# A table load placed ahead of a transfer on ScalarE, and a 1.5 KB transfer moved back in the load queue

## The chip, the core and the metric

One core of a Trainium2 chip runs the kernel, in one launch. The core has five instruction streams that matter here: PE (matrix products and transposes), ACT (ScalarE), DVE (VectorE), POOL (GpSimd) and SP, which only issues transfers. ACT and POOL issue transfers too, from the same stream that gives them their arithmetic. All transfers are carried out by the same 16 DMA engines.

The metric is the device time of one execution in microseconds (us). Three executions of the kernel before took 119.38, 119.49 and 120.67 us, a median of 119.49.

## What is computed

Two stages in one kernel. The first is a linear attention with a decaying state, for 4 batches, 8 heads, 768 steps and a head size of 48. The second takes its output as 3072 rows of 384 and runs a soft mixture of experts (8 experts of 4 slots, hidden size 1024).

```python
# attention: r, k, v are (4, 8, 768, 48); w, u are (8, 48)
for t in range(S):
    cur = einsum('bhd,bhe->bhde', u[None] * k[:, :, t], v[:, :, t])
    y[:, :, t] = einsum('bhd,bhde->bhe', r[:, :, t], state + cur)
    state = w[None, :, :, None] * state + einsum('bhd,bhe->bhde', k[:, :, t], v[:, :, t])
x = y.transpose(0, 2, 1, 3).reshape(3072, 384)
# soft mixture of experts
logits = x @ phi                                   # (3072, 32)
d = softmax(logits, axis=0); c = softmax(logits, axis=1)
slot_in = (d.T @ x).reshape(8, 4, 384)
slot_out[e] = relu(slot_in[e] @ w1[e]) @ w2[e]     # 8 experts
out = c @ slot_out.reshape(32, 384)
```

`w` and `u` are 1.5 KB each. `w` enters everything: its logarithm, times a position, is exponentiated into tables by which every k and r is scaled. `u` enters only the term of a step with itself.

## The kernel before, in words

**Tiling.** The 768 steps are cut into chunks of 128, and a batch is loaded in two parts: a small one (m even, 384 KB for each of k, r and v) and a large one (m odd, 768 KB each). So there are 24 loads, named `Lk0 Lr0 Lv0` to `Lk7 Lr7 Lv7`. Each goes into one of 14 buffers `raw`, all through one function, `load_f` (line 195), issued by SP. The expert weights, 16 matrices of 1.57 MB in float32, are later loaded into the same buffers by POOL (lines 783 and 785), which turns them into bfloat16 on the way, 768 KB each in SBUF. The first of these waits for a small copy (`gate`, line 781) that needs the load `Lk6`.

**The order of the work.** Nothing is scheduled at run time. The string `ORDER` (lines 9 to 31) names some 500 tasks, and `L.run(ORDER)` emits them in that order; each task puts its instructions at the end of its engine's stream, and each engine works its stream off in order. A name with `:ACT` or `:DVE` picks the engine. The first line of the string sets the start:

```python
CB0 Lk0 Sk0 Lr0 Tk0 Sr0 LU Lv0 Ek0:ACT VC0:ACT Lk1 AHa AHb F0_2 Tr0 Lr1 PR0 TB0b F1_3 N0 TB0a F2_2 Tv0 Ev0 Lv1 CC Lk2
```

The tasks that matter here are:

- `LU` (line 381): SP issues the load of `u` into `u_f`, 4 rows of 384 bytes. It stands behind `Lr0`.
- `Sk…`, `Sr…` (line 427): k or r times a table; the first two on DVE, most others on POOL.
- `T…` (line 436): PE turns a scaled tile; `E…` (lines 357 and 359): DVE or ACT copies it out of PSUM; `PR` (452): DVE multiplies; `N`, `V` (481, 491): PE turns tiles again.
- `AHa AHb` (line 281, DVE) and `TB…` (line 397, ACT): arguments and exponentials of the large tables. `Sk1b`, the first product on POOL, needs `TB0b`.
- `CC` (lines 291 to 293): DVE copies a small constant (`permT`), then `w_f`, then `u_f` into `wu`. `CT` (line 311): PE turns both, one transpose each. `CA` (314): DVE copies the result out. `CU` (317, 318; POOL) and `CW` (322, 324; ACT) make `ucol` and `wT` of it, which all later state updates use.
- `F…_n` (line 861): matrix products of n times 256 columns whose result nobody reads.
- The tail: `W15a`, `W15` (line 785) load the last weight matrix in two parts; `Q11`, `Q12`, `Q13` (line 921) are its products, behind which line 928 (ACT) and lines 949 to 955 make and store the output.

**Ahead of the tasks** stands a straight piece of code. ACT's stream begins with these two lines:

```python
O(act.dma_start(out=w_f, in_=w.rearrange("(o q e) d -> o q (e d)", o=1, e=2).to_broadcast([C // nQ, nQ, P2])))   # L211
O(act.preload_act_table_set("natural_log_exp_and_others"))                                                       # L212
```

The first issues the load of `w`, broadcast to 128 rows (48 KB). The second loads the function table that holds logarithm and exponential. Behind them ACT makes two permutation matrices of an identity that POOL writes (lines 255 and 260), then the logarithm of `w` (line 283), then DVE multiplies (281) and ACT exponentiates (287, 288). On PE, 2 and then 7 products on zeros (line 219) stand around two matrix products (266, 267) that need the permutation matrix of line 255.

**Waits of the load queue.** The transfers issued by SP and ACT share eight completion semaphores in turn. So each such transfer from the ninth on waits, ahead of its issue, for the landing of the one eight places before it. In the kernel before the first eight are w, k0, r0, u, v0, k1, r1, v1.

Of the kernel before, what the change touches and what calls it, by code (L numbers as in the profile page):

```python
# [6 lines left out]


ORDER = """
CB0 Lk0 Sk0 Lr0 Tk0 Sr0 LU Lv0 Ek0:ACT VC0:ACT Lk1 AHa AHb F0_2 Tr0 Lr1 PR0 TB0b F1_3 N0 TB0a F2_2 Tv0 Ev0 Lv1 CC Lk2  # L10
TB1b F3a_9 V0 CT Sk1b Sr1b Sk1a:DVE Lr2 Er0:ACT NE0:ACT CA F4a_11 Tk1b F5a_1 Tk1a VE0 A00 CB TB1a Ek1a VC1b VC1a:ACT
Lv2 CU K00 F6_4 Tr1b Tv1a Ek1b:ACT CW Ev1a Lk3 Sr1a F7y_1 U0 Er1b:ACT SM0 Sk2 N2 A01 K01 NE2:ACT Tv1b Sr2 Ev1b:ACT
Sk3a F8y_3 Tr1a SI0 Lr3 Lv3 N1 Sk3b Er1a:ACT Lk4 VC3b PR1b V1 A10 Sr3a DV0 VC2:ACT K10 Y0 NE1:ACT VE1:ACT Sr3b YE0 Tv2
# [68 lines left out]
def kernel(  # L82
# [31 lines left out]
    CC = NS // U3  # L114
# [11 lines left out]
    def O(ins):  # L126
        return tc.keep_in_program_order(ins)

    pe, dve, act, pool, sp = nc.tensor, nc.vector, nc.scalar, nc.gpsimd, nc.sync
# [78 lines left out]
    for t in wu_t:  # L208
        O(dve.memset(t[:], 1.0))

    O(act.dma_start(out=w_f, in_=w.rearrange("(o q e) d -> o q (e d)", o=1, e=2).to_broadcast([C // nQ, nQ, P2])))  # L211
    O(act.preload_act_table_set("natural_log_exp_and_others"))  # L212

    warm = LexpT[:, 0:512]
    O(dve.memset(warm, 0.0))
# [770 lines left out]
```

## Time and profile before

| what | value |
|---|---|
| median of three executions | 119.49 us |
| the profiled execution's own time | 120.24 us |
| its span, first to last instruction | 118.5 us |
| busy share of the span: PE, DVE, ACT, POOL | 83%, 80%, 73%, 52% |
| mean granted clock of PE | 0.962 |
| bytes read from and written to HBM | 39.42 MB, 4.72 MB |

The profile's rows give a start and a duration in us (ns where a row says mean ns), the engine, the line of the kernel, and what was written from what. An engine's name with a q behind it (SPq, ACTq) is its instruction stream, which issues transfers. "DMA share" is the mean busy share of the 16 DMA engines. Rates in GB/s count the bytes moved as written to SBUF; the weights are read as float32 and written as bfloat16, so half the rate stands for the same reading. Rows that end in a releaser in brackets tell how long the engine stood idle and what ended it.

### The profile page before, as it was taken

The page shows a single profiled execution, that of the slowest core. Times are in us where ns is not written, and L with a number is a line of the kernel's source. Part 1 is how long each engine was busy: PE and PEld are TensorE (multiplying, and loading weights), DVE is VectorE, ACT ScalarE, POOL GpSimd, SP SyncE. Part 2 cuts the span into 40 slices and gives each one's busy share as a digit, 9 for nine tenths or more (in the row PEclk, how much of TensorE's full clock was granted, in tenths as well). Part 3 has the DMA queues.
Part 4 walks back from the last instruction along what each step waited for, and adds up shares of the span by engine and source line. Part 5 has one row for each costly group of instructions (what it writes and reads, how often), then busy time and mean ns, then how long its engine had stood idle before and what let it go on. Part 6 is the DMA issues. An engine that isn't in the chain of part 4 may idle for free.

```text
span 118.5 us, 3926 instructions
## 1 busy us (share of the span) xinstructions
PE 98.0 (83%) x1660; PEld 71.1 (60%) x1660; DVE 94.8 (80%) x180; ACT 86.6 (73%) x140; POOL 61.0 (52%) x79
## 2 busy tenths in 40 slices
PE   3997895999999999989999989999899985498000
PEld 0364674787888787867788878686453542254000
DVE  6899987898999999999999989999786274099100
ACT  5769894999999999989899799979644151269000
POOL 7605899999999989999999010002303000000000
PEclk9999999999999999999999999999999999869955
DMA  2999999999999999999999999999999995059994
GB/s 31 333 387 374 364 408 397 383 390 401 384 384 391 297 229 223 219 215 214 217 212 221 210 223 207 223 207 219 212 212 218 216 207 104 12 199 407 419 402 166
DMA packets 10441, 31.81 MB, mean 268 GB/s; under 512 B 1080, under 2 KB 4408, under 8 KB 10424
## 3 DMA queue, kind: packets, MB, share of 16 engines
q0 software_dynamic: 2448, 12.58, 51.8%
q1 hardware_dynamic: 7832, 18.93, 42.3%
q8 instruction: 13, 0.21, 0.7%
q10 hardware_dynamic: 144, 0.05, 0.2%
q14 instruction: 4, 0.03, 0.1%
HBM read 39.42 MB, written 4.72 MB: 373 GB/s over the span
## 4 chain that ended last, share of the span: by engine, by line
PE 32%; DMA 23%; POOL 15%; DVE 9%; ACT 6%; issue 4%; SPq 3%; DVEq 0%; ACTq 0%; POOLq 0%
DMA raw<-in_moe_w_dram 16%; POOL mix L427 12%; PE T L436 7%; DMA raw<-in_r_dram 7%; PE Ab L506 3%; DVE mix L953 2%; PE Yb L572 2%; SPq L195 2%; PE T L491 2%; PE Yb L567 2%; DVE AT_all L511 2%; ACT xT_all L359 2%; PE Yb L578 2%; PE T L481 2%; PE T L595 2%
## 5 line engine op out<-in xcount | busy, mean ns | idle before, releaser
L427 POOL TENSOR_TENSOR mix<-raw,tabl 128x768 bf16<-128x768 f32 x15 | 27.7, 1858 | 5.8 <-ACT tabl L397 5.4
L511 DVE TENSOR_TENSOR AT_all<-Ab,mask 128x1024 bf16<-128x1024 f32 x24 | 29.3, 1219 | 1.1 <-PE Ab L506 0.5
L359 ACT COPY mix<-T 128x1024 bf16<-128x1024 bf16 x19 | 19.1, 1021 | 3.9 <-PE T L436 2.3
L436 PEld LDWEIGHTS <-mix 128*128 128x128 bf16 x192 | 11.8, 99 | 2.3 <-DVE mix L427 0.7
L555 DVE TENSOR_TENSOR dv<-vn,Mb 128x768 bf16<-128x768 bf16 x12 | 11.4, 946 | 1.4 <-PE Mb L545 1.1
L427 POOL TENSOR_TENSOR mix<-raw,tabs 128x768 bf16<-128x768 f32 x6 | 10.8, 1815 | 0.0
L359 ACT COPY vT_all<-T 96x1024 bf16<-96x1024 bf16 x10 | 10.2, 1021 | 0.5 <-PE T L436 0.4
L506 PE MATMUL Ab<-mix 64*128 64x128 bf16 x192 | 9.5, 218 | 1.2 <-ACT mix L359 1.0
L359 ACT COPY xT_all<-T 128x768 bf16<-128x768 bf16 (+1 forms) x12 | 9.3, 784 | 1.3 <-PE T L595 1.3
L359 ACT CAST x<-Yb 128x768 bf16<-128x768 f32 x12 | 9.7, 808 | 0.0
L436 PE MATMUL T<-turnl,mix 128*128 128x128 bf16 x128 | 9.6, 219 | 0.1
L359 ACT COPY vn<-T 128x768 bf16<-128x768 bf16 x11 | 8.8, 814 | 0.0
L452 DVE TENSOR_TENSOR pr<-T,mix 128x1024 bf16<-128x1024 bf16 x12 | 8.0, 681 | 0.0
L712 POOL TENSOR_TENSOR Lc<-Ls,sm 128x192 bf16<-128x192 f32 x2 | 1.0, 516 | 13.5 <-ACT E L690 13.5
L506 PEld LDWEIGHTS <-mix 64*128 64x128 bf16 x192 | 5.8, 94 | 3.5 <-issue 0.7
L572 PEld LDWEIGHTS <-AT_all 128*128 128x128 bf16 x192 | 6.6, 96 | 1.6
L359 ACT COPY kn<-T 128x768 bf16<-128x768 bf16 (+1 forms) x10 | 7.2, 722 | 0.1
L418 POOL CAST vj<-raw 128x768 bf16<-128x768 f32 x8 | 6.7, 832 | 0.6 <-POOL phi_s L336 0.6
L436 PEld LDWEIGHTS <-vj 128*96 128x96 bf16 x96 | 6.2, 123 | 1.2 <-issue 0.2
L572 PE MATMUL Yb<-vn,AT_all 128*128 128x48 bf16 x192 | 6.8, 183 | 0.0
L539 DVE TENSOR_TENSOR Z<-Mb,wT 128x384 bf16<-128x384 f32 x12 | 6.6, 553 | 0.1
L481 PE MATMUL T<-ident,mix 128*128 128x128 bf16 x80 | 6.1, 219 | 0.2
(187 smaller groups left out, 237.8 us busy)
## 6 DMA issues: line engine op xcount, KB each, us to landing
raw<-in_moe_w_dram POOLq DMA_DIRECT2D x13, 768.0 KB, 14.4
raw<-in_k_dram SPq DMA_DIRECT2D x4, 768.0 KB, 12.2
raw<-in_r_dram SPq DMA_DIRECT2D x4, 768.0 KB, 12.2
raw<-in_v_dram SPq DMA_DIRECT2D x4, 768.0 KB, 12.2
out_dram<-mix SPq DMA_DIRECT2D x3, 768.0 KB, 4.6
raw<-in_k_dram SPq DMA_DIRECT2D x4, 384.0 KB, 10.9
raw<-in_r_dram SPq DMA_DIRECT2D x4, 384.0 KB, 10.6
raw<-in_v_dram SPq DMA_DIRECT2D x4, 384.0 KB, 10.8
```

The lines of the kernel that those rows point to most:

```text
L195: O(sp.dma_start(out=dst[:, 0:2 * jn * D].rearrange("p (e x) -> p e x", e=2), in_=a[b].rearrange("h (y j) d -> y h (j d)", j=jn)[lg * CC * ...
L359: O(act.copy(dst, src))
L418: O(act.copy(o, i_) if t.eng == "ACT" else pool.tensor_copy(o, i_))
L427: O(eng.tensor_mul(src.inst.rearrange("p (j e s) -> p e j s", j=JH, e=2)[:, :, :, 0:D], rv(), tab))
L436: O(pe.transpose(Tb.inst[0:P, jj * 128:(jj + 1) * 128], sv[:, jj, :], (turn, turnl)[lg][:]))
L452: O(dve.tensor_mul(cv(pb), tv(), cv(kT)))
L481: O(pe.transpose(Tb.inst[:, x * 128:(x + 1) * 128], kT.inst[:, x, :], ident[:]))
L506: O(pe.matmul(Abf.inst[:, e, x * C:(x + 1) * C], kT.inst[s, g * nQ + x, :], rT.inst[s, g * nQ + x, :]))
L511: O(dve.tensor_mul(AT.inst[:], Abf.inst[:].rearrange("p e (g t) -> p e g t", g=nQ), mask[:, None, None, :].to_broadcast([128, 2, nQ, C])))
L539: O(dve.tensor_mul(Smid.inst[:], Mf.inst[:, 0:SW].rearrange("p (q d) -> p q d", q=nQ)[:, :, None, :].to_broadcast([128, nQ, 2, D]), wT[:, ...
L555: O(dve.tensor_mul(dvb.inst[:].rearrange("p g e d -> p (g e) d"), vn.inst[:].rearrange("p g e d -> p (g e) d"), Mf.inst[:, 448:448 + 2 * P ...
L572: O(pe.matmul(y[:, x // nQ, q * P2 + e * D:q * P2 + (e + 1) * D], a[x // nQ].inst[:, e, q, :], vn.inst[:, x, e, :], start=False, stop=(c = ...
```

## The change

Two edits. The load of the function table is put ahead of the issue of `w` in ACT's stream. `LU` goes from behind `Lr0` to behind `Lv1`, so that SP issues `u` as the seventh of its loads instead of the third. In the instruction lists of the two kernels PE, DVE and POOL have the same instructions in the same order; only ACT's first two are exchanged, and SP's `u` stands behind v0, k1, r1 and v1.

```diff
 ORDER = """
-CB0 Lk0 Sk0 Lr0 Tk0 Sr0 LU Lv0 Ek0:ACT VC0:ACT Lk1 AHa AHb F0_2 Tr0 Lr1 PR0 TB0b F1_3 N0 TB0a F2_2 Tv0 Ev0 Lv1 CC Lk2
+CB0 Lk0 Sk0 Lr0 Tk0 Sr0 Lv0 Ek0:ACT VC0:ACT Lk1 AHa AHb F0_2 Tr0 Lr1 PR0 TB0b F1_3 N0 TB0a F2_2 Tv0 Ev0 Lv1 LU CC Lk2
...
-    O(act.dma_start(out=w_f, in_=w.rearrange("(o q e) d -> o q (e d)", o=1, e=2).to_broadcast([C // nQ, nQ, P2])))
     O(act.preload_act_table_set("natural_log_exp_and_others"))
+    O(act.dma_start(out=w_f, in_=w.rearrange("(o q e) d -> o q (e d)", o=1, e=2).to_broadcast([C // nQ, nQ, P2])))
```

The semaphores follow the issue order. After the change the first eight of the shared turn are k0, r0, w, v0, k1, r1, v1, u; so the waits of the eight loads behind them change (k2 waits for k0 instead of w, r2 for r0 instead of k0, v2 for w instead of r0, k3 for v0 instead of u, r3 for k1 instead of v0, v3 for r1 instead of k1, k4 for v1 instead of r1, r4 for u instead of v1), and from v4 on they are the same as before.

More of the change, by code (lines that the diff above doesn't have):

```diff
@@ L209 @@
         O(dve.memset(t[:], 1.0))
+    O(act.preload_act_table_set("natural_log_exp_and_others"))
     O(act.dma_start(out=w_f, in_=w.rearrange("(o q e) d -> o q (e d)", o=1, e=2).to_broadcast([C // nQ, nQ, P2])))
-    O(act.preload_act_table_set("natural_log_exp_and_others"))
     warm = LexpT[:, 0:512]
```

## The prediction, made before the changed kernel ran

> **What bounds the kernel now.** I read the slices of the span first, then the end of the chain of work, then the transfers by line, and at last the start in order of time. The slices say that the 16 DMA engines are full from the second slice to the 33rd, and again while the output is written:
>
> ```profile
> DMA  2999999999999999999999999999999995059994
> GB/s 31 333 387 374 364 408 397 383 390 401 384 384 391 297 229 223 219 215 214 217 212 221 210 223 207 223 207 219 212 212 218 216 207 104 12 199 407 419 402 166
> ```
>
> (The fall from 390 to 215 GB/s at 40 us is the expert weights, which count half for what is read.) The chain that ended last hangs its long middle piece on the issue of `W15a`, the last weights but one:
>
> ```profile
> 82.28 0.46 POOL Lc L712
> 82.73 18.82 DMA raw<-in_moe_w_dram
> 101.60 0.51 PE Yb L921 x7
> ```
>
> That reads as if POOL's work ahead of 82.73 set the end. The transfers say otherwise (count, KB, us from issue to landing):
>
> ```profile
> tabl<-in_moe_w_dram POOLq DMA_DIRECT2D x1, 768.0 KB, 30.1
> ...
> raw<-in_moe_w_dram POOLq DMA_DIRECT2D x1, 672.0 KB, 18.8
> ```
>
> The 768 KB ahead of it were issued at 68.23 and landed 30.1 us later, at 98.3; `W15a` landed at 82.73 + 18.82 = 101.55, 3.2 us behind, about what 688 kB take at 215 GB/s. So it queued until some 98 us, and could have been issued several us later for the same landing. The bound is the transfer stream from 2.4 us to 101.6, then the output. Work on the other engines matters only if it is late at the end, and there it has room:
>
> ```profile
> PE Yb L861 <- POOL mix L427: 1.3, 1, 1.3
> ...
> PE Yb L921 <- DMA raw<-in_moe_w_dram: 2.2, 1, 2.2
> ```
>
> PE stood idle for 2.17 us before its last products, for weights alone (the other idle time, 1.28 us at 19.80, is used below). The output's copies of `LexpT` were done at 99.0, four us before their use.
>
> **The start**, where both edits lie:
>
> ```profile
> 0.73 0.63 ACTq L211 DMA_DIRECT2D LexpT<-in_w_dram  x1
> ...
> 1.39 1.28 ACT L212 ACT_TABLE_LOAD   x1 [1.39 <-PEq L970]
> ...
> 2.35 0.53 SPq L381 DMA_DIRECT2D LexpT<-in_u_dram  x1
> ...
> 2.69 0.42 ACT L255 COPY idp<-ident 128x128 bf16<-128x128 bf16 x1
> ...
> 3.43 0.28 ACT L283 ACTIVATE LexpT<-LexpT 128x96 f32<-128x96 f32 x1
> ...
> 10.68 1.65 DVE L293 COPY wu<-LexpT 4x96 f32<-4x96 f32 x2
> ...
> 12.48 2.39 POOL L427 TENSOR_TENSOR mix<-raw,tabl 128x768 bf16<-128x768 f32 x1 [0.34 <-DMA raw<-in_r_dram]
> ```
>
> **Part 1, the table load ahead of w.** Before, the table load could begin only when the issue of w ended (0.73 + 0.63 = 1.36, began 1.39), and line 255 behind it at 2.69. Exchanged, the table load begins at 0.75 and ends at 2.03, so lines 255 and 260 come 0.64 us earlier if w's issue does not hold them up. Gain to the logarithm (283): it needs w, which landed 2.7 us after its issue, at 3.43, the moment at which it began. So the 0.64 ends in a wait for w: gain 0.
>
> The open question is when w is issued. The trace has no transfer behind arithmetic on ACT. Lower bound: at once, 0.05 behind the table load, w at 3.45, loss 0. Upper bound by the nearest row, POOL, whose issues begin only as the operation in front ends:
>
> ```profile
> 43.03 3.60 POOL L427 TENSOR_TENSOR mix<-raw,tabl 128x768 bf16<-128x768 f32 x2
> 46.56 0.59 POOL L783 DMA_DIRECT2D raw<-in_moe_w_dram  x1
> ```
>
> By that row w is issued at 2.03 and lands at 4.73, 1.3 us late, or some 0.5 more, since its 128 small rows would then share the engines with k0 and r0 (the DMA share is 0.63 from 2 to 3 us and 0.98 from 3 to 4). I take the middle for the start, 0.6 us late, as POOL's issue is made by the engine's own work (0.59 busy) and ACT's need not be; both ends stay in the range. From line 283 on there is no slack: 283, 281, 287, the products on DVE, 281 again, `TB0b`, and POOL's first product at 10.33 follow one another, so the whole arithmetic would shift by this amount, less 0.34 which POOL waited for r1 at 12.48 anyway. What hides it is the 2.17 us at the end. Price: 0 with that cover, the shift less 2.17 without.
>
> On this the Trainium skill has a rule. "PSUM — Partial Sum Buffer", section "Engine vs sequencer instructions", says that the stream's own instructions wait only until the earlier ones are handed to the engine, not until they are complete; by it w would go out under the table load and land at about 3.45. The sum would be the same by the rule and by POOL's row; no run here shows ACT's case yet.
>
> **Part 2, u three loads and one more behind.** SP loses 0.53 + 0.04 us between r0 and v0, so v0, k1, r1, v1 are issued 0.56 us earlier, u at about 5.1, and k2 at 5.67 as before. The bytes are the same and the DMA engines are at 0.95 to 1.06 from 3 us on, so earlier issues mostly queue. The only thin place is 5.0 to 5.75 us, where the rate was 277, 258 and 326 GB/s against 390; filling it is worth 77 kB or 0.2 us at most. I take half: 0.1 us earlier for all that follows in the stream, the end included. The bounds are 0 and 0.2.
>
> u itself had only k0 and r0 in front of it. Now it stands behind v1, which landed 9.4 us after its issue at 4.87:
>
> ```profile
> raw<-in_v_dram SPq DMA_DIRECT2D x1, 768.0 KB, 9.4
> ```
>
> That is 14.27. Landings keep the order of issue here (r1 12.35, v1 14.27, k2 15.37), so u lands between 12.4 and 15.4; I take 14.2. DVE copied u at 12.1, so it waits about 2.1 us (0.3 to 3.3). Behind it on DVE stand `Sk1a`, `CA`, the copy for `VE0` and the memory sets of `CB`; on PE, `CT` (12.26 before), six fillers and the turns of k1 (13.73); on ACT the copies of k1 (15.15). All go some 2 us late. POOL does not: its next need of this chain is `CU` at 15.60, and `CA` would be done at about 15.5. POOL is what PE waits for at 19.80, by 1.28 us, so PE is then 0.8 us behind, and at the end 0.8 of 2.17 us is used. Price on the end: 0, with a cover of 1.28 + 2.17 = 3.45 us for a wait of 2.1.
>
> The load queue: each load waits for the one eight places ahead (k4 issued 12.37, r1 landed 12.35; r4 14.32, v1 14.27). After the change v3 waits for r1 (11.30 becomes 12.4) and k4 for v1 (12.37 becomes 14.2), r4 for u (as before); v4 is unchanged. When k4 is issued, k2, r2, v2, k3, r3, v3 are still out, 3456 KB or 9 us at 390 GB/s, so the stream does not run dry. Price 0; it would cost about 1 us only if less than that were out. The weights' gate at 35.42 is set by POOL, and a shift of 1 us there falls into a stream that still holds v7 (issued 31.08, landed 50).
>
> **Sum.** 0 (table load) - 0.1 (earlier loads) + 0 (u late) + 0 (queue) = -0.1 us. On the profiled execution, 118.5 us of span in 120.24, that is 120.1; the median of the runs lies 0.75 below that execution, so the forecast is 119.49 - 0.1 = 119.4 us. Within 1% (1.2 us) a measurement of this kernel can hardly be told from no change.
>
> **Rivals.**
>
> *A, slower: u's wait lets PE's clock fall.* PE was idle from 11.14 to 12.26. With u at 14.2 it is idle for 3.2 us. At the end of the kernel idle PE lost its clock:
>
> ```profile
> 99.50:100.00 0.50, 0.00 (x0) 0.00 (x0) 0.00 (x0) 0.00 (x0) 0.00 (x0) 1.00 0.40 72
> ...
> 103.00:103.50 0.50, 0.50 (x3) 0.44 (x3) 0.00 (x0) 0.14 (x1) 0.00 (x0) 0.50 0.12 33
> ```
>
> (The number before the DMA share is the clock.) After 2.17 idle us and a short burst it fell to 0.50 at 102.7 and stayed until 106.2. The same at 14 us would cost half of 3.5, 1.75 us, on top of the 2.1: 3.85 against a cover of 3.45, an end 0.4 later, 119.9. If u lands at 15.4 it is 1.2 more, 121.1. It decides from a total of 3.45 on. For it: PE's turns of k1 stand right behind. Against it: the idle time is at the edge of what the trace shows to suffice, and lost clock is made up wherever PE waits. The skill's "TensorE: Matmul & The Clock Gate", "What's actually happening", puts the idle window at about 3.4 us, which this gap only just reaches; the fall at 102.7 came 3.3 us after PE went idle, so the trace agrees.
>
> *B, faster: late arithmetic keeps PE warm at the end.* If PE's last products before the wait come 1 us later, the idle time shrinks to about 1.1 us and the clock may hold; the first output products then take 0.16 instead of 0.32 us each, and the output transfers, full only from 105.5, begin some 0.6 earlier: 118.8. Against it: it needs a shift that survives 80 us of other waits.
>
> *C, the first edit does what POOL's row says.* w is held by 1.3 to 1.8 us, all arithmetic shifts by 1.0 to 1.5, the end still waits for weights: 119.4 to 119.5, no other time than the forecast. Only above 2.17 would it show.
>
> **How the numbers follow.** Forecast with C, end set by the weights: 0.68, 119.1 to 119.7. A: 0.20, of which 0.13 end above 120.7 (slower by over 1%). B: 0.12, of which 0.05 reach below 118.3. So faster 0.05, within 1% 0.82, slower 0.13. The runs before spread by 0.1 below to 1.2 above their median, which I add at the top: the range is 118.7 to 120.7, leaving out 0.13 above (A) and 0.07 below (B).
>
> **What would show it.** Right: the last `L921` again waits for weights at about 101.5; the DMA row is full from the second slice; `L293` lasts until 14 us or more; the table load begins near 0.75. Part 1 is decided by where ACTq's issue of w stands against the table load. Wrong: `L921` at the end released by PE, DVE or ACT instead of DMA (A), the clock below 1.0 near 15 us (A), or a hole in the DMA share between 12 and 45 us, which would break the main premise.

## The result, and the profile after

| | before | after |
|---|---|---|
| median, 22 executions of each on one chip | 119.36 us | 120.55 us |
| ratio of the two, 95% interval | | 1.0096 [1.0073, 1.0119] |
| the profiled execution's own time | 120.24 us | 120.25 us |
| its span; mean granted clock | 118.5 us; 0.962 | 118.4 us; 0.976 |

The changed kernel is slower by some 1.15 us (119.36 × 0.0096). The two profiled executions show none of that, and the first thing to read is why: neither is typical. Before's lies 0.9 us above its kernel's median. After's lies 0.3 below its own, and its clock of 0.976 is the highest of the 22. Ratios, intervals and counts, here and below, leave out executions over 1.5% above the fastest of the same kernel (two of the 22 of after), while medians keep them. Of after's 20 counted executions 17 have a mean clock below 0.9585. So this profile is read for the start and for where things wait, and the time is explained by experiments.

The slices of the span of after. The third row is the rate in GB/s; the two rows above it are in tenths:

```profile
PEclk9999999999999999999999999999999999999955
DMA  2999999999999999999999999999999995159994
GB/s 29 297 334 412 392 390 399 383 391 399 383 388 392 322 227 224 214 217 214 214 213 220 211 218 213 218 213 218 209 216 214 219 210 112 19 195 410 419 409 166
```

The DMA engines are full over the same slices as before, but the second and third slice move 297 and 334 GB/s where before moved 333 and 387. The start of after, in order of time (start, duration, engine, line; in brackets the idle time before and what ended it):

```profile
0.73 1.28 ACT L211 ACT_TABLE_LOAD   x1 [0.73 <-PEq L970]
0.75 0.64 ACTq L212 DMA_DIRECT2D LexpT<-in_w_dram  x1
2.02 0.42 ACT L255 COPY idp<-ident 128x128 bf16<-128x128 bf16 x1
...
2.37 0.61 SPq L195 DMA_DIRECT2D raw<-in_v_dram  x1
3.29 0.28 ACT L283 ACTIVATE LexpT<-LexpT 128x96 f32<-128x96 f32 x1 [0.45 <-DMA LexpT<-in_w_dram]
4.98 0.89 SPq L381 DMA_DIRECT2D LexpT<-in_u_dram  x1
9.69 0.83 ACT L418 CAST vj<-raw 128x768 bf16<-128x768 f32 x1 [1.42 <-DMA raw<-in_v_dram]
11.72 4.55 POOL L427 TENSOR_TENSOR mix<-raw,tabl 128x768 bf16<-128x768 f32 x2 [6.78 <-DMA raw<-in_k_dram]
12.06 1.65 DVE L293 COPY wu<-LexpT 4x96 f32<-4x96 f32 x2
```

Three things stand there. The issue of w (0.75) begins 0.02 us behind the table load's start, not behind its end. v0 is issued at 2.37, 0.54 earlier than before, and ACT waits for it until 9.69, so it took 7.3 us to land; before it took 4.6. And `L293`, the copies of w and u, have no wait for u: what stands ahead of them was already later by v0's delay (their start went from 10.68 to 12.06), which hid u's.

The chain and the waits at the end of after, to be held against before's 82.28, 82.73, 101.60 and 2.2:

```profile
84.12 17.93 DMA raw<-in_moe_w_dram
102.09 0.51 PE Yb L921 x7
```

```profile
PE Yb L921 <- DMA raw<-in_moe_w_dram: 1.3, 1, 1.3
```

The last weights but one landed at 84.12 + 17.93 = 102.05, 0.5 later than in before's profile, and still PE waited for them. The span came out equal all the same: the output stage kept its clock here (1.00 from 102 to 106 us), where in before's profile it fell to 0.50 at 102.7.

### The profile page after: what moved, and what is told of

Same layout as the page of the kernel before. It is cut to its first block, busy times and chain, and to the rows that moved or that the text cites. A ratio compares the mean times of both kernels' runs of the same rounds, so it can differ in the third digit from the quotient of the medians.

```text
span 118.4 us, 3925 instructions
## 1 busy us (share of the span) xinstructions
PE 97.5 (82%) x1660; PEld 71.0 (60%) x1660; DVE 94.2 (80%) x180; ACT 86.9 (73%) x140; POOL 61.2 (52%) x79
## 4 chain that ended last, share of the span: by engine, by line
PE 38%; DMA 21%; DVE 10%; ACT 10%; POOL 7%; issue 3%; SPq 1%; DVEq 0%; POOLq 0%; ACTq 0%
DMA raw<-in_moe_w_dram 15%; PE T L436 9%; DMA raw<-in_v_dram 6%; POOL mix L427 6%; PE Ab L506 4%; DVE mix L953 3%; PE Yb L572 3%; PE Yb L567 3%; PE Yb L578 2%; PE T L481 2%; PE Mb L532 2%; PE T L595 2%; PE Mb L529 2%; PE T L491 2%; DVE AT_all L511 2%
## 5 line engine op out<-in xcount | busy, mean ns | idle before, releaser
L359 ACT COPY vT_all<-T 96x1024 bf16<-96x1024 bf16 x10 | 10.2, 1021 | 0.6 <-PE T L436 0.4
L712 POOL TENSOR_TENSOR Lc<-Ls,sm 128x192 bf16<-128x192 f32 x2 | 1.0, 516 | 13.6 <-ACT E L690 13.6
```

The source lines that it names most:

```text
L359: O(act.copy(dst, src))
```

## The experiments

My theory after this look was that rival A is at work in the executions that were not profiled: u is late at its use, PE stands idle and the clock falls. The first rival to it was that the loads without u's issue between them run slower, as the rates suggest. The second was that the table load costs something. Each kernel below ran 12 times (`i3_u_later_still` six times) beside the kernel before on the same chip. "Low clock" counts executions with a mean granted clock below 0.9585, a bound chosen after the result to part the two groups of after; of the kernel before, 1 to 3 of 23 to 33 are below it in each of the four batches.

### One edit at a time, and the gap put back

`e1_table_only` has the exchange of the two ACT lines alone. `e2_u_only` has `LU` behind `Lv1` alone. `e3_spacer` is the changed kernel with a load of 1.5 KB that nobody reads at u's old place, so that the time between the issues of r0 and v0 is as before:

```diff
-... Lk0 Sk0 Lr0 Tk0 Sr0 Lv0 ...
+... Lk0 Sk0 Lr0 Tk0 Sr0 LS Lv0 ...
+    spare = cst.tile([nQ, P2], f32, name="spare")
+    add("LS", "SP", lambda t: O(sp.dma_start(out=spare[:], in_=u.rearrange("(q e) d -> q (e d)", e=2))))
```

`e4_u_on_act` is the changed kernel with u early but no gap: ACT issues it behind w, SP not at all.

> The table load ahead of w, u at its old place. Theory P (the gap that u's issue left between r0 and v0 is what mattered): v0 lands about 4.6 us after its issue as before, the transfers keep 390 GB/s but for 5 to 6 us, time within 0.3 us of before (119.4). Theory T (the table load ahead, or w's issue under it, does the harm): v0 lands 7 us or more after its issue, the rate falls below 300 GB/s from 5 to 7 us, time 1.0 to 1.2 us above before. Theory U (u landing late on DVE does the harm): as before, 119.4.

> u behind the second v, the table load behind w as before. Theory P: v0 lands about 7.3 us after its issue, the rate is below 300 GB/s for two us from 5 us on, time 1.0 to 1.2 us above before (120.5). Theory T: as before, 119.4. Theory U: 120.5, and DVE's copies of line 293 last 2 us or more.

> The changed kernel, with one more 1.5 KB load of u into an unused tile at u's old place between r0 and v0; the u that is used stays late. Theory P: the gap is back, so v0 lands after about 4.6 us and the time is that of before, 119.2 to 119.7. Theory T or U: as the changed kernel, 120.4 to 120.7.

> The changed kernel with u issued by ACT right behind w, so that SP issues only k, r and v, with no gap, and u lands early. Theory P: still slow, v0 lands after 7 us, 120.3 to 120.7. Theory U: u is there in time, 119.2 to 119.6. Theory T: slow, as the changed kernel.

| kernel | median (before 119.48) | ratio, 95% | low clock |
|---|---|---|---|
| e1_table_only | 119.79 | 1.0032 [1.0002, 1.0061] | 0 of 12 |
| e2_u_only | 120.26 | 1.0070 [1.0044, 1.0096] | 9 of 12 |
| e3_spacer | 119.96 | 1.0029 [0.9992, 1.0066] | 7 of 10 |
| e4_u_on_act | 120.12 | 1.0044 [1.0007, 1.0080] | 0 of 10 |

The low clock goes with the late u: it is there in e2 and e3, where u is late, and in none of e1 and e4, where it is not. The time does not follow as simply. e1 and e2 came out about where theory U had put them. e3 had 119.2 to 119.7 us from P and 120.4 to 120.7 from U and lies between, and e4 lies between its two forecasts as well. e3 differs from e1 in the lateness of u alone, with the gap kept in both, and e3 over e1 is 0.9998 [0.9966, 1.0031] (means of the counted executions, interval by resampling them, as in all such pairs below): no cost is seen there.

e2's profile shows what the wait does. First DVE, PE and POOL in order of time:

```profile
14.11 0.20 DVE L293 COPY wu<-LexpT 4x96 f32<-4x96 f32 x1 [1.86 <-DMA LexpT<-in_u_dram]
```

```profile
12.30 0.22 PE L311 MATMUL Yb<-ident_f,wu 4*128 4x4 f32 x1 [0.89 <-DVE wu L293]
14.36 0.22 PE L311 MATMUL Yb<-ident_f,wu 4*128 4x4 f32 x1 [1.84 <-DVE wu L293]
14.51 1.89 PE L861 MATMUL Ab<-mix,ident 128*128 128x512 bf16 x6
16.20 1.06 PE L436 MATMUL T<-turnl,mix 128*128 128x128 bf16 x8
...
20.07 0.27 PE L861 MATMUL Yb<-mix,ident 128*128 128x256 bf16 x1
```

```profile
16.38 1.81 POOL L427 TENSOR_TENSOR mix<-raw,tabl 128x768 bf16<-128x768 f32 x1
20.43 1.82 POOL L427 TENSOR_TENSOR mix<-raw,tabs 128x768 bf16<-128x768 f32 x1 [2.24 <-PE Yb L861]
```

Before, the turns of k1, the same filler and the same POOL product:

```profile
13.73 0.61 PE L436 MATMUL T<-turnl,mix 128*128 128x128 bf16 x8
...
16.49 0.27 PE L861 MATMUL Yb<-mix,ident 128*128 128x256 bf16 x1
```

```profile
17.94 3.57 POOL L427 TENSOR_TENSOR mix<-raw,tabs 128x768 bf16<-128x768 f32 x2
```

Then the stretches of one us in e2 (behind PEld, DVE, ACT and POOL come the clock, the DMA share and the rate):

```profile
13.00:14.00 1.00, 0.00 (x0) 0.00 (x0) 0.00 (x0) 1.00 (x2) 1.00 (x1) 1.00 1.07 389
...
15.00:16.00 1.00, 1.00 (x5) 0.32 (x4) 0.90 (x4) 0.13 (x1) 1.00 (x2) 0.60 1.09 387
16.00:17.00 1.00, 1.00 (x10) 0.93 (x9) 0.65 (x3) 0.00 (x0) 0.85 (x3) 0.50 1.04 390
17.00:18.00 1.00, 1.00 (x11) 0.93 (x9) 0.00 (x0) 0.71 (x1) 1.00 (x1) 0.50 1.04 406
```

DVE stands 1.86 us for u, and PE does nothing but one 0.22 us transpose for 2.9 us (0.89 + 0.22 + 1.84). Then PE's clock is at 0.5 to 0.6 for three us, and the eight turns of k1 take 1.06 us instead of 0.61. They begin 2.47 us later than before, and the filler at 20.07 is 3.58 us later. POOL's product, which this filler releases, is 2.49 us later (20.43 against 17.94): before, PE waited 1.28 us for POOL at this place; here POOL waits 2.24 us for PE. From there the lateness stays. POOL's `L712`, which was at 82.28, comes at 84.79, and the end of e2 is

```profile
101.44 0.51 PE L921 MATMUL Yb<-tabl,AT_all 128*32 128x384 bf16 x8
101.78 0.58 PE L921 MATMUL Yb<-raw,AT_all 128*32 128x384 bf16 x8
```

The rows show no wait for weights any more. But the room is only just used up: the last of these products begins at about 102.0, as the last 96 KB of weights land (91.84 + 10.2 = 102.04). In e3's profile, where the clock is at 0.5 from 13.2 to almost 20 us, the arithmetic does set the end. The last two pieces of its chain are PE's products alone:

```profile
100.90 0.83 PE Yb L923 x16
102.71 0.82 PE Yb L923 x16
```

All its weights had landed at 93.04 + 8.7 = 101.74, and the eight products that need the last two pieces began at 102.97, 1.2 us later.

e1 gives the issue of w a second look:

```profile
0.74 1.28 ACT L211 ACT_TABLE_LOAD   x1 [0.74 <-PEq L970]
0.77 0.62 ACTq L212 DMA_DIRECT2D LexpT<-in_w_dram  x1
2.04 0.42 ACT L255 COPY idp<-ident 128x128 bf16<-128x128 bf16 x1
...
3.42 0.28 ACT L283 ACTIVATE LexpT<-LexpT 128x96 f32<-128x96 f32 x1 [0.55 <-DMA LexpT<-in_w_dram]
```

The logarithm begins at 3.42, against 3.43 before: neither gain nor loss. Its 1.0032 therefore has no place in the profile; the control below reads 1.0023.

### Each suspect alone on the kernel before, with a control

`g1_before_again` is the kernel before, unchanged, run as if it were a new one. `g2_late_u_alone` is the kernel before with the unread load at u's old place and `LU` behind `Lv1`: late u, gap kept. `g3_no_gap_alone` has u issued by ACT behind w: gap gone, u early. `g4_u_behind_v0` moves `LU` by one load only:

```diff
-... Lr0 Tk0 Sr0 LU Lv0 Ek0:ACT ...
+... Lr0 Tk0 Sr0 Lv0 LU Ek0:ACT ...
```

> The kernel before once more, as a second look at its profile and as a measure of what the comparison itself gives: every theory expects 1.000 within 0.003; v0 lands 4.3 to 4.7 us after its issue, and the last products wait for weights between 100.5 and 101.6 us.

> The kernel before (table load behind w), with an unused 1.5 KB load at u's old place and the u that is used behind the second v: only u's lateness is left of the change. Theory U: DVE's second copy of line 293 waits 1 to 2 us for u, all arithmetic is 1.5 to 3.5 us later, the last products no longer wait for weights or hardly, time 0.4 to 1.0 us above before. Theory P (the gap): v0 in time, full rate, time within 0.3 us of before. A theory of both (the stream loses 0.5 us by the missing gap, the arithmetic loses up to 3 us by u, and the later of the two decides): 0.2 to 0.6 us above before.

> The kernel before (table load behind w's and u's issues), with u issued by ACT behind w, so that u is early and SP has no gap between r0 and v0: only the missing gap is left of the change. The table load comes 0.7 us later than before, which line 283 may feel by about 0.6 us. Theory P: rate below 300 GB/s for two us from 5 us on, v0 lands 5.8 us or more after its issue, the weights land 0.5 us later, time 0.3 to 0.8 us above before. Theory U: within 0.3 us of before.

> The kernel before with u one place later, behind the first v: the gap now lies between v0 and k1, and u lands with v0, some 3 us ahead of its use. Theory P, if it is the place of the gap between r0 and v0 that matters: slow stretch as in the changed kernel, v0 lands 5.8 us or more after its issue, time 0.3 to 0.8 us above before. Theory P, if any gap among the first loads does: as before, 119.2 to 119.7. Theory U: as before.

| kernel | median (before 119.97) | ratio, 95% | low clock |
|---|---|---|---|
| g1_before_again | 120.38 | 1.0023 [0.9987, 1.0059] | 3 of 11 |
| g2_late_u_alone | 120.39 | 1.0045 [1.0009, 1.0080] | 9 of 11 |
| g3_no_gap_alone | 119.64 | 0.9997 [0.9959, 1.0035] | 0 of 12 |
| g4_u_behind_v0 | 119.46 | 0.9955 [0.9916, 0.9994] | 0 of 10 |

The control reads 0.2% slow, so that much here is noise, and e1's 0.3% cannot be told from it. Against the kernel before the late u is slower and the missing gap is not. But g2 over the control is 1.0003 [0.9970, 1.0038]: with the gap kept, the late u again shows no cost. g2 over g3 is 1.0044 [1.0010, 1.0079], and in the first batch e2 over e1 is 1.0039 [1.0013, 1.0063], but in each of these two pairs the gap differs as well as u. One difference is in the profiles: with the gap kept DVE waits for u 0.94 us (e3) and 1.46 us (g2), without it 1.86 (e2).

### The late u kept, its wait taken away

`h4_use_later` is the changed kernel with the tasks that use u put further back; every transfer is issued as in the changed kernel:

```diff
-... Lv1 LU CC Lk2
-TB1b F3a_9 V0 CT Sk1b Sr1b Sk1a:DVE Lr2 Er0:ACT NE0:ACT CA F4a_11 Tk1b F5a_1 Tk1a VE0 A00 CB TB1a ...
+... Lv1 LU Lk2
+TB1b F3a_9 V0 Sk1b Sr1b Sk1a:DVE Lr2 Er0:ACT NE0:ACT F4a_11 Tk1b F5a_1 Tk1a VE0 A00 CB CC CT CA TB1a ...
```

`h1_filler_ahead` is the changed kernel with only the fillers `F4a_11` in front of `CT`, so that PE is idle for less time while DVE waits as long. `h2_changed_again` is the changed kernel a second time, and `h3_table_and_u_behind_v0` has g4's place for u and the table load ahead.

> The changed kernel with the filler of 11 units (six matrix products that nobody reads, 1.4 us) moved ahead of the transposes that wait for u, so that PE is idle for under 2 us there instead of over 3. Same work on every engine. If the fall of PE's clock behind the wait for u carries the loss (rival A): clock 1.0 from 12 to 20 us, mean clock 0.965 or more in most executions, and 0.4 to 0.8 us less than the changed kernel. If the late u costs by the wait alone, or the missing gap in the stream does: within 0.3 us of the changed kernel.

> The changed kernel once more, for a second profile, since its mean clock (0.976) was not that of most of its executions (0.95), and as the partner of the others on this chip. Rival A expects a profile with DVE waiting 1 to 2 us for u, PE's clock at 0.5 for some 3.5 us from 13 to 15 us on, and last products that hardly wait for weights; time 0.7 to 1.3 us above before. The missing gap alone expects the clock at 1.0 and the last products waiting for weights at 102 us.

> The first edit as it is, the second reduced to one place: u behind the first v instead of the second, so that u lands with v0, 3 us ahead of its use, and a gap is left between v0 and k1. If the lateness of u and the missing gap carry the loss: no wait for u, clock 1.0, 119.0 to 119.6 when before is at 119.5, within 0.4% of before. If the table load carries part of it: 0.3 us above before.

> The changed kernel's transfers unchanged, u late, but its use moved back: DVE's copies, PE's two transposes and the copy out come behind the products of chunk 0 instead of ahead of the turns of k1. Then nothing waits for u, and PE is not idle there. If u's lateness at its use is what costs: 0.5 to 1.0 us less than the changed kernel, the missing gap left alone. If the missing gap is what costs: within 0.3 us of the changed kernel.

| kernel | median (before 119.62) | ratio, 95% | low clock |
|---|---|---|---|
| h1_filler_ahead | 120.40 | 1.0041 [1.0000, 1.0081] | 2 of 10 |
| h2_changed_again | 120.21 | 1.0052 [1.0013, 1.0091] | 7 of 12 |
| h3_table_and_u_behind_v0 | 119.80 | 1.0011 [0.9974, 1.0048] | 0 of 12 |
| h4_use_later | 119.71 | 1.0004 [0.9963, 1.0045] | 0 of 11 |

With the same transfers and the use put back, the slowdown is gone: h2 over h4 is 1.0045 [1.0008, 1.0081], half a us. (h4 also changes the order of a few tasks on DVE and PE.) In h4 PE is busy where e2's was empty:

```profile
13.00:14.00 1.00, 0.99 (x16) 0.67 (x14) 0.89 (x3) 1.00 (x2) 1.00 (x1) 1.00 1.05 391
...
16.00:17.00 1.00, 1.00 (x11) 0.75 (x12) 0.80 (x3) 0.90 (x4) 0.40 (x2) 1.00 1.04 393
```

h1 parts the wait from the clock only in sign: the low clock became rarer (2 of 10 against 7 of 12), and the time is not told from h2's (h2 over h1: 1.0020 [0.9981, 1.0061]). h2's profile shows the forecast wait, and that the clock need not fall after it:

```profile
11.14 0.19 DVE L293 COPY wu<-LexpT 4x96 f32<-4x96 f32 x1
13.33 1.63 DVE L293 COPY wu<-LexpT 4x96 f32<-4x96 f32 x1 [2.00 <-DMA LexpT<-in_u_dram]
```

```profile
15.01 0.22 PE L311 MATMUL Yb<-ident_f,wu 4*128 4x4 f32 x1 [3.24 <-DVE wu L293]
...
19.12 0.27 PE L861 MATMUL Yb<-mix,ident 128*128 128x256 bf16 x1
...
101.79 0.86 PE L921 MATMUL Yb<-raw,AT_all 128*32 128x384 bf16 x8 [0.40 <-DMA raw<-in_moe_w_dram]
```

```profile
19.48 3.59 POOL L427 TENSOR_TENSOR mix<-raw,tabs 128x768 bf16<-128x768 f32 x2 [0.64 <-PE Yb L861]
```

PE is idle for 3.24 us and keeps clock 1.0. The filler is then 2.63 us later than before and POOL's product 1.54; the room at the end has shrunk to 0.40 us, and this execution took 119.92, faster than the kernel's median. With the clock lost as well, as in e2's profile, none is left.

### More of the same wait, and the gap without it

`i3_u_later_still` puts u behind v2 in the changed kernel, behind three more loads of 384 KB, a larger dose of the wait. `i1_no_gap_use_later` is e2 with h4's later use, so without a gap and without a wait; `i2_gap_use_later` is i1 with the unread load in the gap. `i4_u_behind_k1` is the kernel before with `LU` behind `Lk1`.

> Transfers as with the second edit alone (u behind the second v, no gap between r0 and v0; the table load behind w as before), u used later on DVE and PE so that little waits for it. If the missing gap costs: 0.3 to 0.6 us above before and above the next kernel. If only u's lateness costs: within 0.3 us of before and of the next kernel, mean clock 0.965 or more.

> The kernel before this one in the list with an unused 1.5 KB load between r0 and v0, so that the gap is back; u as late, used as late. If the missing gap costs: 0.3 to 0.6 us less than without it, at the time of before. If only u's lateness costs: the same as without it, within 0.3 us.

> The changed kernel with u behind the third v of the load queue (v2) instead of the second (v1); every other instruction in its place, and the missing gap as it was. u then lands at about 17.2 us instead of 14.2, so DVE's wait grows from 2 to 5 us. If u's lateness carries the loss: the growth of 3 us meets a cover that is used up, so 2 to 3.5 us above the changed kernel, 122 to 124, the last products no longer waiting for weights. If the missing gap carries it: as the changed kernel, 120.2 to 120.6.

> The kernel before with u two places later, behind k1; the table load behind w as before. u lands with k1 at about 10, just ahead of its use at 10.9 to 12.2, so it costs no wait. If u's lateness carries the loss: within 0.3 us of before, mean clock 0.965 or more, though the stream shows the slow stretch. If the missing gap does: 0.3 to 0.6 us above before.

| kernel | median (before 120.12) | ratio, 95% | low clock |
|---|---|---|---|
| i1_no_gap_use_later | 119.74 | 0.9966 [0.9931, 1.0001] | 0 of 10 |
| i2_gap_use_later | 119.96 | 0.9935 [0.9894, 0.9976] | 0 of 6 |
| i3_u_later_still | 123.00 | 1.0220 [1.0177, 1.0262] | 6 of 6 |
| i4_u_behind_k1 | 119.82 | 0.9982 [0.9947, 1.0018] | 0 of 12 |

(i2's ratio counts six of its twelve executions, and its profile was taken of one of the others and is not used.) The dose answers: in i3 the wait is twice as long, every execution has the low clock, and the loss is 2.2%. The slices, and the two instructions in order of time:

```profile
PEclk9999965799999999999999999999999999999855
DMA  2999999999999389999999999999999999139994
```

```profile
16.98 0.20 DVE L293 COPY wu<-LexpT 4x96 f32<-4x96 f32 x1 [3.74 <-DMA LexpT<-in_u_dram]
```

```profile
17.23 0.26 PE L311 MATMUL Yb<-ident_f,wu 4*128 4x4 f32 x1 [3.72 <-DVE wu L293]
```

Here the stream itself breaks too (the 3 in the DMA row): the copy that opens the weights, `L781`, came at 41.64 instead of 35.42, and from 41 to 43 us the DMA share is 0.07. So i3 is more than a pure dose of A. Its last products began at 105.46 and had no wait for weights.

Put together, the ratios to the kernel before speak for both conditions at once. Without the gap, four kernels in which u is late at its use read 1.0096 (after), 1.0070 (e2), 1.0052 (h2) and 1.0041 (h1), and five in which u is early or used later read 1.0044 (e4), 1.0004 (h4), 0.9997 (g3), 0.9982 (i4) and 0.9966 (i1). With the gap kept, the late u reads 1.0029 (e3) and 1.0045 (g2), beside 1.0032 (e1) and 1.0023 (g1) with u in time. So the cost of the late use is shown where the gap is missing, and is not seen where it is kept, though the intervals there allow up to 0.3 and 0.4%.

**The gap.** The rate from 5 us on shows what its loss does to the stream. These are stretches of half a us; the last three columns are clock, DMA share and GB/s. After:

```profile
5.00:5.50 0.50, 0.50 (x2) 0.15 (x1) 0.46 (x3) 0.50 (x2) 0.00 (x0) 1.00 1.26 240
5.50:6.00 0.50, 0.50 (x2) 0.00 (x0) 0.50 (x1) 0.50 (x2) 0.00 (x0) 1.00 0.83 209
6.00:6.50 0.50, 0.34 (x3) 0.17 (x3) 0.50 (x2) 0.17 (x2) 0.00 (x0) 1.00 0.87 286
6.50:7.00 0.50, 0.50 (x8) 0.50 (x6) 0.50 (x1) 0.00 (x0) 0.00 (x0) 1.00 1.00 280
```

Before:

```profile
5.00:5.50 0.50, 0.50 (x2) 0.15 (x1) 0.39 (x3) 0.50 (x2) 0.00 (x0) 1.00 0.98 267
5.50:6.00 0.50, 0.50 (x2) 0.15 (x1) 0.50 (x1) 0.50 (x1) 0.00 (x0) 1.00 0.98 335
6.00:6.50 0.50, 0.50 (x3) 0.03 (x2) 0.50 (x2) 0.31 (x2) 0.00 (x0) 1.00 1.05 396
6.50:7.00 0.50, 0.50 (x7) 0.50 (x7) 0.50 (x1) 0.00 (x0) 0.00 (x0) 1.00 1.04 418
```

After moves 200 kB less in two us ((27 + 126 + 110 + 138) GB/s × 0.5 us). In every profile with no issue between r0 and v0 nor right behind v0 (after, e2, e4, g3, h1, h2, h4, i1, i3, i4) the rate is low there and v0 needs 5.6 to 7.3 us from its issue; in before, e1, e3, g1 and g2, which have one between r0 and v0, 4.3 to 4.7; and in g4 and h3, with u right behind v0, 5.0. At the end the price is small and not settled: held against each other, e4 over e1 is 1.0019 [0.9990, 1.0051], e2 over e3 1.0040 [1.0009, 1.0070], i1 over i2 1.0055 [1.0030, 1.0082], but g3 over the control 0.9959 [0.9927, 0.9993], the other way. e2 and e3 also differ in the table load. i1 over i2 rests on the six counted executions of i2; the means of all twelve of each are 120.06 us for i1 and 120.21 for i2, the other way.

**A better version?** g4 and i2 read 0.4% and 0.6% below the kernel before, on chips where that kernel read 119.97 and 120.12 and not 119.4. The same place for u together with the table load (h3) reads 1.0011. None is shown to beat the kernel before.

## Why the prediction was wrong, point by point

The forecast was 119.4 us and no change that could be told from noise; after measured 120.55 beside 119.36. That this lies inside the range of 118.7 to 120.7 is owed to the 1.2 us that were added at the top for the spread of executions, not to the sum.

**Table load: right, at nothing.** w's issue went out at 0.75 under a table load that lasts until 2.01, so it was 0.02 and not 0.6 us late, and POOL's row was no guide to ACT. The Trainium skill's "PSUM — Partial Sum Buffer", section "Engine vs sequencer instructions", says of instructions that the sequencer itself executes (its examples are a nop and semaphore operations) that they wait only for the dispatch of earlier ones, not for their completion. The trace agrees for this issue of a transfer, which the section does not name. The 0.67 us by which line 255 began earlier ended in a wait for w (0.45 in after, 0.55 in e1), as the prediction said.

**Earlier loads: the rate went the other way.** The term had bounds of 0 and 0.2 us of gain and allowed no loss, since "earlier issues mostly queue". They queue and also run slower: 200 kB less from 5 to 7 us, worth 200 kB / 390 GB/s = 0.5 us at full rate. Whether that reaches the end is not settled. In after's profile the last weights but one landed 0.5 us later (102.05 against 101.55), but over the profiles whose last products waited for weights these began at 101.06 (h1) to 102.28 us (g3) without the gap and at 101.06 (e1) to 101.60 (before) with it.

**u late: this is the step that decided.** The wait was forecast at 2.1 us and measured at 1.86 (e2) and 2.00 (h2). The price of 0 rested on "a cover of 1.28 + 2.17 = 3.45 us for a wait of 2.1". The first part of the cover was sized about right: between PE's filler and POOL's product 1.1 us of the lateness went (3.58 to 2.49 in e2, 2.63 to 1.54 in h2). Two other things failed. What had to be covered was not 2.1: by their mean clock, most executions of the changed kernel lost clock there, and with it PE was 3.6 us late in e2's profile; the forecast left this to rival A. And 2.17 was one execution's room. The kernel before run again (g1) has 1.46, and kernels with u in time have 0.89 (e1) to 2.59 (h3). The forecast let 0.8 us reach the end; 1.54 (h2) and 2.49 us (e2) came out behind POOL. (Of these 0.46 and 0.26 stood ahead of u: DVE's copies of line 293 began at 11.14 and 10.94 instead of 10.68.) That left 0.40 us of room in h2's profile and none in e2's, and e3's products began 1.2 us behind the last weights. With the gap missing, the price was not 0 but about half a us (h2 over h4).

Rival A named this mechanism and gave 119.9, but only with a chance of 0.20, with "lost clock is made up wherever PE waits" and the idle time "at the edge" against it. The fall at 102.7 was weaker support than the prediction made of it: of the 3.3 us between PE's going idle and the fall PE had worked 0.84 (`L921`, 101.60 to 102.44).

How much of the loss is the wait and how much the clock is not settled. e2's executions with low clock have a median of 120.28 us, and the three others 120.25; h2's have 120.75 and 120.08. e3 and g2 have the low clock in most executions too (7 of 10, 9 of 11) and are no slower than e1 and g1. So the low clock is a sign of the wait more than a proved cause of the time. Why the wait costs nothing that can be seen with the gap kept stays open as well; that u lands earlier then, and that the weights may, are two possible reasons that no run here parts.

**The queue: right.** The DMA row of after is full from the second slice to the 33rd, and PE's last products still waited for weights in its profile. The premise breaks only at the larger dose (i3).

**Rival B** was seen in single executions: after's profile has its arithmetic 1.4 us later (82.28 to 83.66), a shorter wait for weights and a full clock in the output stage, and its span equals before's though its weights landed later. But the kernel before keeps that clock in other executions as well (0.974 in g1's profile, with 1.46 us of wait), so it is no gain of the change.

**The sizes.** After was 0.96% slower beside its own 22 executions of before and 0.52% in h2; with the control at 0.23%, the change costs about 0.5 to 1%. Of that, u's lateness at its use is 0.45% where the gap is missing (h2 over h4, the one pair that differs in the wait with the same transfers), and the table load nothing that can be seen. Whether the rest is noise, or the missing gap, the runs do not settle.

## What to carry to other kernels

A small transfer issued behind large ones waits for most of their bytes (u, issued at 5.04 in e2, landed at about 14.1, and v1 ahead of it at 14.2): move it only with the date of its first use at hand, and ask who stands idle behind that wait and for how long. Ask also what that idle time does to the engine's clock, and add it to what has to be covered. Before the room at the end of one profile is spent, compare that execution's own time and clock with those of the other executions; here the room was 2.17 us in the one profile, 1.46 in a second one of the same kernel, and 0.89 to 2.59 in kernels like it.

## What the runs showed of the hardware that was not expected

- Six loads issued by SP without a small one between the second and the third, nor right behind the third, move 221 (i3) to 286 GB/s (i1) between 5 and 7 us, where with a 1.5 KB load between the second and the third they move 354 (before) to 365 (e1, g2). With it right behind the third it is 335 (g4) and 304 (h3). The mean DMA share over these two us is 0.86 (h2) to 1.00 (g3) without and 1.01 (before) to 1.04 (g2) with the load in between, and after has 0.99: in each of them the bytes fall by more than the share does. The unread load brings back v0's short landing as u's own does (4.3 us in e3), so it is the issue or its time that counts, and not whether anything waits for what is loaded. Why the same loads move fewer bytes no run here shows.
- The small load does not strictly keep its place. In after's profile DVE had copied u by 13.71, and v1, issued ahead of it, landed only at about 15.6, when ACT's wait for it ended.
- The same idle time of PE does not always cost the clock. In h2's profile 3.24 us idle left it at 1.0. In i3's it fell at 15.8 us, 2.3 us into the idle time of 3.72; in e3's at 13.2, within an idle time of 2.9 us that held one 0.22 us transpose; in e2's at 15.2, 0.9 us after PE had begun to work again. The Trainium skill's "TensorE: Matmul & The Clock Gate", section "What's actually happening", has an idle window of about 3.4 us and calls it free-running, so that the same kernel can come out differently. The 3.2 us that the prediction forecast do not just reach it, as it said, but fall short. h2 agrees with the window, and that 7 of its 12 executions have the low clock and its profiled one has not agrees with the free-running. i3 agrees only if the transpose ahead of its idle time did not count as work, which was not tried. e2 and e3 do not agree even then: e2's PE was without a full product for 2.95 us (from 10.90 + 0.51 = 11.41 to 14.36), and e3's clock fell 2.1 us behind its last one (10.54 + 0.51 = 11.05).
- At the end of the kernel the length of the last wait for weights went with the clock of the output stage: 1.65 us (g3) or less left it at 1.0 from 102 to 106 us, and 1.69 (i4), 2.17 (before) and 2.59 us (h3) were followed by 0.5.
